# v beside a block of ones in one product with phi(k), and n of chunks 4 to 7 turned by VectorE and DRAM instead of TensorE

## Chip, cores and metric

The kernel runs on one core of a Trainium2 chip. The metric is the device time of one execution in microseconds (us), as the median of the timed executions; smaller is better.

## The reference

One block of a transformer, in float32, for S = 2048 rows, D = 512 columns, H = 32 heads of 16 and a hidden width F = 1376. `mod` holds six vectors made from a small input `c`.

```python
h = layernorm(x) * (1 + ca) + sa
q, k, v = split(h @ wqkv)                       # 32 heads of 16
phi(t) = concat(softmax(t @ w_phi), softmax(-t @ w_phi))      # 32 features a head
kv = phi(k)^T v ;  z = sum over the rows of phi(k)            # a head: 32 x 16, and 32
o = (phi(q) kv) / (phi(q) . z + 1e-6)
x = x + ga * (o @ wo)
h = layernorm(x) * (1 + cb) + sb
n = layernorm(h)
x1 = h + shifted(gelu(n @ w1)) @ w2             # column quarters shifted by +1, -1, +2, -2 rows
x = x + gb * (x1 + gelu(layernorm(x1) @ w3) @ w4)
```

## The kernel before

The 2048 rows are 16 tiles of 128 rows, in 8 chunks of two tiles. Large products are made of three float32r matmuls each (high times high, high times low, low times high), so each operand is split into a high and a low part by `hi_lo` (an ACT or VectorE copy and a subtraction).

**Stage 1, the loop over chunks of lines 802 to 826.** For each chunk `h_chunk` makes h turned (feature by row) with TensorE transposes, `k_feat`, `v_feat` and `q_feat` make a tile's phi(k), v and phi(q) (phi(q) goes to DRAM), and `kv_add` (line 783) adds phi(k)^T v of a tile into the PSUM tile `kva`. There, an item is 32 columns of v (two heads) against 64 columns of phi(k) (their features): 16 items a tile, on the four 32-column strips of the array, each in float32 and so two matmul instructions. Half of each product belongs to two different heads and is masked away later with `block` (line 840). The sum z is made apart: line 790 adds phi(k) of the tiles 0 to 14 into `za` on VectorE or GpSimd, and lines 844 to 847 sum `za` and phi(k) of tile 15 over the partitions by two sets of matmuls with ones; `zbc` holds z on all partitions. `kvb` (lines 833 to 840) is kv turned by matmuls with the identity.

**Stage 2, `phase_a` for each chunk** (line 909) and `mix` (line 1009). `q_phi` loads phi(q), multiplies by `zbc` (tiles `ez`), sums, divides and turns it by VectorE (`pT`). The products `num` (phi(q) kv, 64 x 32 strips of the array), `o` (with wo), two layernorms (tiles `h`, `n`), then n is turned by `to_T` (line 861: four 128x128 TensorE transposes a tile into PSUM `pt`, and `hi_lo` from there into `nT`), then `g` (with w1, gelu) and in `mix` the product `x` with w2. Beside it `split_w3` prepares combinations of w3 and stores them to DRAM.

**Stage 3, `block`**: the last MLP by a Strassen-like scheme: products `u` (with w3, PSUM `pa`) and `b` (with w4, PSUM `ac`). Its operand is turned in another way, by `normed` (line 1118): VectorE turns 32x32 blocks (`turn`), `store_rows` writes the two tiles to DRAM, and `load_turned` fetches them back with the blocks in place, in four DMAs. For that, the ACT pass that normalises writes its columns in a permuted order (`mixed`).

**What sets the order.** Every operation gets a number as the Python code creates it. `ORDER` (line 40) lists these numbers: it is the order in which operations are emitted, and so the order of each engine's own queue (a letter behind a number picks the engine where there is a choice). `SLOT` gives each tile its buffer. The costs that stand beside the operations in the code have no effect when the kernel runs; only these two tables have. The SP queue issues nearly all DMAs, in the same order. So an instruction that waits holds up everything that stands behind it on its engine.

On TensorE, with a name for each operation by its step and tile (k, v, q, kv of tiles 0 to 15; num and g of chunks 0 to 7, o, n and x by tile; z, kvb, w2: small products on strips of the array), the order before has the strip products in these runs: w2; kv0 to kv3; kv4 to kv6; kv7; kv8 to kv11; both z and kv12 to kv14; kv15; kvb; num0; num1 in two runs; num2 to num7 in one run each. From z to num0 it reads: z z kv12 kv13 kv14 q8 v15 q9 kv15 q12 kvb q10 num0.

Of the kernel before, what the change touches and what calls it, by code (L numbers as in the profile page):

```python
# [11 lines left out]
OP = mybir.AluOpType  # L12
# [3 lines left out]
P = 128  # L16
NK = D // P
HG = 64 // DH
# [16 lines left out]
        "s4": ("mod2", "ke", "qe", "e", "ez", "pT", "gf", "gg", "bH", "bL", "wr", "za", "tw"),  # L35
        "s2": ("raw", "rk", "ws", "tr", "cu", "mod", "acc", "bd", "xl", "xn", "h", "n", "xb", "xc", "gb", "vv", "kvs", "qt", "yt", "sg", "gl", "uu", "nb"),
# [128 lines left out]
)  # L165
SLOT = {
    "pp": "510234426360573046405216574732325716511600313075732270653365216523706542035040435752736700267672"
          "4243153510404460571",
    "bd": "46",
    "w": "134625cd387165ad28cb09",  # L170
    "rk": "73958dgc",
# [1216 lines left out]
```

## Time and profile before

| | us |
|---|---|
| median of 3 timed executions | 554.73 |
| lowest, highest | 554.42, 555.75 |
| profiled execution, first to last instruction (span) | 552.9 |
| median less span: what lies around the first and last instruction | 1.8 |
| TensorE (PE) busy in the span | 544.9 |
| VectorE (DVE) | 488.6 |
| ScalarE (ACT) | 351.7 |
| GpSimd (POOL) | 344.5 |

The profile gives no time of its own for the profiled execution beside its span; the three timed executions stand for it. In the profile, a line such as `L471` is the line of the kernel; `mms` at 471 emits nearly all matmuls, so groups are told apart by their tiles (`kva<-ke,vv` is the sum of phi(k)^T v, `pt<-const,n` the transposes of n). The span falls into three parts: 0 to about 160 us is stage 1, 160 to about 345 us stage 2 with the first products of stage 3 mixed in, and the rest stage 3.

### The profile page before, as it was taken

Reading aid. Unit: us, or ns where it says so; the run is one execution under the profiler, and the core shown is the slowest. Engines: PE = TensorE matmul, PEld = TensorE weight load, DVE = VectorE, ACT = ScalarE, POOL = GpSimd, SP = SyncE. Lnnn points to the kernel's source line nnn. Section 1 sums busy time; section 2 is a strip of 40 time slices with the busy share of each in tenths; the row PEclk is TensorE's granted clock in tenths of the full one; section 3 lists DMA queues with packets and bytes.
Section 4 is the critical chain, followed back from the end, with each engine's and each line's share of the span. In section 5 each row is a group of like instructions: output and inputs, shape, how many; then the busy total and the mean of one; then the engine's idle time right before and its main releaser. Section 6 shows DMA issues by size and latency. Waiting matters only on the chain.

```text
span 552.9 us, 12370 instructions
## 1 busy us (share of the span) xinstructions
PE 544.9 (99%) x4498; PEld 488.1 (88%) x4498; DVE 488.6 (88%) x903; ACT 351.7 (64%) x828; POOL 344.5 (62%) x351
## 2 busy tenths in 40 slices
PE   8999999999989999999999999999999999999997
PEld 7888788878767788888889898999999999999996
DVE  3999999899999999999998878987888868896886
ACT  2899898834436788969888877866434543434540
POOL 2499985979599999978886545234150434254442
PEclk9999999999999999999999999999999999999999
DMA  8982544537736766869987878986689673872022
GB/s 323 392 277 89 175 170 137 176 112 248 205 118 226 249 195 206 275 235 319 292 275 270 242 257 301 339 356 231 284 248 347 245 284 97 264 286 80 25 92 95
DMA packets 63749, 124.90 MB, mean 226 GB/s; under 512 B 7140, under 2 KB 26852, under 8 KB 59592
## 3 DMA queue, kind: packets, MB, share of 16 engines
q1 hardware_dynamic: 63400, 124.04, 66.4%
q8 instruction: 35, 0.57, 0.4%
q14 instruction: 26, 0.21, 0.1%
q10 hardware_dynamic: 288, 0.07, 0.1%
HBM read 89.74 MB, written 34.35 MB: 224 GB/s over the span
## 4 chain that ended last, share of the span: by engine, by line
PE 86%; DVE 7%; POOL 3%; DMA 2%; issue 1%; ACT 0%; DVEq 0%; POOLq 0%
PE pp L471 36%; PE pa L471 27%; PE ac L471 20%; PE pt L480 2%; DVE pz L442 2%; DVE q L442 2%; DMA mod<-in_wmod 1%; PE kva L471 1%; POOL qe L420 1%; DVE pT L762 1%; POOL ez L420 1%; POOL e L420 1%; DVE ez L418 1%; DMA const<-in_c 1%; DVE pp L437 0%
## 5 line engine op out<-in xcount | busy, mean ns | idle before, releaser
L471 PE MATMUL pp<-w,hh 128*128 128x512 f32 x576 | 138.8, 397 | 0.0
L471 PEld LDWEIGHTS pp<-w,hh 128*128 128x128 f32 x576 | 106.7, 188 | 26.1 <-issue 1.6
L471 PE MATMUL pa<-bH,wq 128*128 128x256 f32 x840 | 106.7, 281 | 0.0
L471 PE MATMUL ac<-w,gg 128*128 128x256 f32 x840 | 106.6, 281 | 0.0
L471 PEld LDWEIGHTS ac<-w,gg 128*128 128x128 f32 x840 | 103.4, 189 | 1.1
L471 PEld LDWEIGHTS pa<-bH,wq 128*128 128x128 f32 x840 | 103.1, 189 | 0.9
L471 PE MATMUL pp<-w,sh 128*128 128x512 f32 x192 | 49.4, 399 | 0.0
L471 PE MATMUL pa<-nT,w 128*128 128x256 f32 x384 | 48.3, 282 | 0.8 <-DVE nT L418 0.7
L471 PEld LDWEIGHTS pa<-nT,w 128*128 128x128 f32 x384 | 46.8, 188 | 2.5 <-DVE nT L418 1.2
L471 PE MATMUL pp<-w,oT 128*128 128x512 f32 x192 | 47.4, 395 | 0.0
L471 PEld LDWEIGHTS pp<-w,oT 128*128 128x128 f32 x192 | 35.4, 188 | 8.1 <-DVE oT L418 0.7
L401 ACT ACTIVATE gg<-cu 128x256 fp32r<-128x256 f32 (+1 forms) x56 | 19.1, 359 | 35.1 <-PE ac L471 19.7
L471 PEld LDWEIGHTS pp<-w,sh 128*128 128x128 f32 x192 | 34.6, 188 | 7.5 <-issue 0.8
L588 POOL TENSOR_TENSOR rs<-mv,const 128x2 f32<-128x2 f32 x31 | 23.8, 769 | 25.3 <-ACT mv L595 23.7
L401 ACT ACTIVATE cu<-pa 128x512 f32<-128x512 f32 (+1 forms) x42 | 21.5, 519 | 27.6 <-PE pa L471 22.3
L420 POOL TENSOR_TENSOR gg<-cu,gg 128x128 fp32r<-128x128 f32 (+1 forms) x26 | 15.8, 615 | 33.2 <-ACT gg L401 13.9
L420 POOL TENSOR_TENSOR ez<-e,const 128x1024 f32<-128x1024 f32 x12 | 29.2, 2433 | 5.2 <-DMA dram<-qe 5.1
L401 ACT ACTIVATE gg<-sg 128x512 fp32r<-128x512 f32 x38 | 23.1, 624 | 14.0 <-POOL sg L420 6.0
L420 POOL TENSOR_TENSOR e<-e,q 128x1024 f32<-128x1024 f32 x15 | 28.8, 1938 | 0.4 <-DVE q L418 0.2
L418 DVE TENSOR_TENSOR gg<-cu,gg 128x256 fp32r<-128x256 f32 (+1 forms) x54 | 22.1, 416 | 7.6 <-PE ac L471 4.6
L418 DVE TENSOR_TENSOR gg<-sg,gg 128x512 fp32r<-128x512 f32 x36 | 26.0, 722 | 3.0 <-PE ac L471 1.5
L420 POOL TENSOR_TENSOR ke<-ke,k 128x1024 f32<-128x1024 f32 x14 | 27.2, 1952 | 1.2 <-DVE k L445 1.2
(214 smaller groups left out, 1211.5 us busy)
## 6 DMA issues: line engine op xcount, KB each, us to landing
wq<-dram SPq DMA_DIRECT2D x32, 1024.0 KB, 7.8
dram<-ws SPq DMA_DIRECT2D x35, 256.0 KB, 3.1
xl<-in_x SPq DMA_DIRECT2D x32, 256.0 KB, 4.1
dram<-qe SPq DMA_DIRECT2D x16, 512.0 KB, 3.7
e<-dram SPq DMA_DIRECT2D x64, 128.0 KB, 3.2
raw<-in_w SPq DMA_DIRECT2D x18, 256.0 KB, 3.7
mod<-in_wmod SPq DMA_DIRECT2D x16, 256.0 KB, 5.2
dram<-xl SPq DMA_DIRECT2D x16, 256.0 KB, 3.0
```

The source lines that it names most:

```text
L401: nc.scalar.activation(o(), i(), func, **kw)
L418: dve = ("DVE", 71 + 1.04 * o.n + 90 * (isps(a) and isps(b)), lambda: nc.vector.tensor_tensor(o(), a(), b(), op=op))
L420: pool = ("Pool", cost, lambda: nc.gpsimd.tensor_tensor(o(), a(), b(), op=op))
L442: plan.op("DVE", 65 + 1.04 * a.n + 110 * isps(o), lambda: nc.vector.tensor_reduce(o(), a(), axis=AX.X, op=op), [o], [a])
L471: nc.tensor.matmul(o(), a(), b(), start=s, stop=e, **kw)
L480: nc.tensor.transpose(o(), i(), ident())
L588: plan.op("Pool", 540 + 10 * m, lambda: nc.gpsimd.tensor_tensor(r(), v(), mhalf[:, :m](), op=OP.pow), [r], [v, mhalf])
L762: plan.op("DVE", 71 + 1.04 * o.n, lambda: nc.vector.transpose(o(), i()), [o], [i])
```

## The change

**v beside ones.** v lives in one of three buffers `vz` of 32 heads by 32 columns, whose upper 16 columns of each head are set to 1 once by GpSimd; `v_feat` copies v into the lower 16. An item of `kv_add` is now one head: its 32 columns (v and ones) against its 32 features, 32 items a tile on the four strips. Rows 16 to 31 of each head's 32x32 block of `kva` thereby hold z. The 14 additions into `za`, and `za` itself, are gone. `zbc` comes from `kvs`, the copy of the finished `kva`, by 16 items with a 0/1 matrix `pick`, in place of the two sets with ones; `kvb` comes from 8 items, and the mask is applied to a broadcast of its first 16 columns. Where there were 16 buffers for v, `v_feat` of a tile now writes over the buffer of the tile three before it.

**n turned through DRAM.** For the chunks 4 to 7, the ACT pass writes n in the permuted order, and `turned_block` does with n what `normed` did for stage 3: VectorE `turn`, two stores, four loads, into a new tile `zt`. `nT` is split from there instead of from PSUM. 32 of the 64 transposes of n, and 8 PSUM tiles, are gone.

**Order and buffers anew.** `ORDER` and `SLOT` are replaced as a whole. On TensorE the strip products now stand in these runs: w2; kv0; kv1; kv2 and kv3; kv4; kv5 and kv6; kv7 and kv8; kv9 and kv10; kv11 to kv13; kv14, kv15 and z; kvb; num0 to num3 one run each; num4, num5 two runs each; num6; num7 two runs. From z to num0 it reads: z q6 q10 q11 q8 kvb q9 q15 num0. GpSimd's last step for phi(k), the multiplication by the reciprocal sum, stands in the list directly ahead of kv2, kv4 and kv9 with no work for TensorE between. At the start the transposes of the first chunk come ahead of the third and fourth load of `mod`, where one half stood behind the fourth and the other behind a transpose of `mod`. Steps of `split_w3` begin early in stage 1. The cost written beside a matmul on a strip has its floor changed from 56 to 30, without effect when the kernel runs.

```diff
-    kva = T("kva", [P, NG // 2, P // 2])
-    zacc = T("za", [P, 2 * D])
-    first = []
+    kva = T("kva", [P, NG, 2 * DH])
+    plan.at("vz")
+    vz = [T("vz", [P, H, 2 * DH]) for _ in range(BIAS["vz"])]
+    for v in vz:
+        plan.op("Pool", 700, lambda v=v: nc.gpsimd.memset(v[:, :, DH:](), 1.0), [v[:, :, DH:]])
     def kv_add(e, vv, tt_):
         plan.at(f"kv{tt_}")
-        mms([(kva[32 * (g % 4):32 * (g % 4) + 32, g // 4, :], vv[:, 32 * g:32 * (g + 1)], e[:, 64 * g:64 * (g + 1)],
-              tt_ == 0 and g < 4, tt_ == NT - 1 and g > 2 * NG - 5) for g in range(2 * NG)],
-            [kva], [vv, e], skip=True, tiles=4)
-        first.append(e)
-        if tt_ and tt_ not in BIAS["zpe"]:
-            tt(zacc, first[0] if tt_ == 1 else zacc, e, OP.add, "any")
+        items = []
+        for i, a in np.ndindex(NG, 4):
+            h = 16 * (i // 4) + 2 * (4 * (i % 2) + a) + i // 2 % 2
+            items.append((kva[32 * a:32 * (a + 1), i, :], vv[:, h, :], e[:, 2 * DH * h:2 * DH * (h + 1)],
+                          tt_ == 0 and i == 0, tt_ == NT - 1 and i == NG - 1))
+        mms(items, [kva], [vv, e], skip=True, tiles=4)
...
-    mms([(p[64 * (i // 2):64 * (i // 2) + 64, half * (i % 2):half * (i % 2 + 1), :], kvs[:, i, :], ident.re("p (a x) -> p a x", (half, 2 * DH), a=half), True, True)
-         for i in range(half)], [p], [kvs, ident], tiles=2)
+    mms([(p[32 * (i // 2):32 * (i // 2) + 32, 4 * (i % 2):4 * (i % 2) + 4, :], kvs[:, i, :], ident.re("p (a x) -> p a x", (4, 2 * DH), a=4),
+          True, True) for i in range(NG)], [p], [kvs, ident], skip=True, tiles=4)
...
-    parts = [zacc] + [e for t, e in enumerate(first) if t in BIAS["zpe"]]
-    for n, e in enumerate(parts):
-        mms([(p[32 * a:32 * (a + 1)], ones[:, :32], e.re("p (r f a y) -> p r f a y", (2, NG, 2, 2 * DH), r=2, a=2, y=2 * DH)[:, a // 2, :, a % 2], n == 0,
-              n == len(parts) - 1) for a in range(HG)], [p], [ones, e], skip=True, tiles=4)
+    mms([(p[32 * b:32 * (b + 1)].re("p (u a) f -> p u a f", (2, 4, 2 * DH), u=2)[:, :, a, :], pick[:, a, :], kvs[:, 2 * b:2 * b + 2, :], True, True)
+         for a in range(4) for b in range(4)], [p], [pick, kvs], skip=True, tiles=4)
...
+    def turned_block(xs):
+        z, yd = T("zt", [P, CH // 32, NK, 32]), T("dram", [TPC * P, D])
+        for t, x in enumerate(xs):
+            y = T("yt")
+            turn(y, x)
+            store_rows(yd, t, y)
+        load_turned(z, yd)
+        return z
...
             for i, t in enumerate(ts_):
-                act(ns[t], hs[t], scale=r[:, i:i + 1], bias=nmr[:, i:i + 1])
-                sl = slice(t * P, (t + 1) * P)
-                to_T(ns[t], nT[:, 0, :, sl], nT[:, 1, :, sl])
+                if c not in BIAS["nturn"]:
+                    act(ns[t], hs[t], scale=r[:, i:i + 1], bias=nmr[:, i:i + 1])
+                    sl = slice(t * P, (t + 1) * P)
+                    to_T(ns[t], nT[:, 0, :, sl], nT[:, 1, :, sl])
+                    continue
+                act(*mixing(ns[t], hs[t]), scale=r[:, i:i + 1], bias=nmr[:, i:i + 1], alts=("DVE",))
+        if c in BIAS["nturn"]:
+            z = turned_block(ns)
+            zp = z.perm("p a k j -> p k a j", (1, 0, 2))
+            for j in range(2):
+                ks = slice(2 * j, 2 * j + 2)
+                hi, lo = (nT[:, i, ks, :].re("p k (a j) -> p k a j", (2, CH // 32, 32), j=32) for i in range(2))
+                hi_lo(hi, lo, zp[:, ks], lo_eng="either")
```

More of the change, by code (lines that the diff above doesn't have):

```diff
@@ new lines @@
+    "xn": "200b19hcab3k6263",
+    "mod": "0ea58dgi94hlka0ib1",
+    "mod2": "0123",
+    "kva": "0",
+    "vz": "381",
+    "hh": "487487de",
+    "pt": "126534152332132374573543",
+    "raw": "b67bg2d1aichdcl9463h94e3kjek",
+    "k1": "0044322032214153",
+    "ke": "5029675064907640",
+    "k2": "1042434324123520",
+    "qe": "7469560119615037",
+    "q1": "2000400051320334",
+    "qt": "a42784d07e4g",
+    "acc": "d162k",
+    "kvs": "g",
+    "pz": "0",
+    "q2": "01200023",
+    "e": "5279860289382068",
@@ new lines @@
+    "ez": "0303338367779393",
+    "q3": "3300002222330000",
+    "q5": "35423333",
+    "pT": "1557381068933276",
+    "oT": "87d11444",
+    "nT": "0de77ee0",
+    "n": "4gac9a49818kk5f5",
+    "h": "87d06bf2d31ab82c",
+    "gf": "70779559",
+    "sh": "501e1379",
+    "pa": "464747424205037245173231047014523646712756343651442037660205",
+    "wr": "24645",
+    "ws": "748b4e4f8hb0j35ab48egi7141a560iafc2",
+    "zt": "7775",
+    "yt": "1e785fhhakifigh4a11f28fe",
+    "gb": "l",
+    "tw": "13741",
@@ new lines @@
+    "bL": "26030597",
+    "nb": "8a1ifid7d79dfkk6",
+    "bH": "89840482924568142417091818628684",
+    "tr": "5ig1fc1h4jk4bi83",
+    "wq": "5705e5ea7b5a7bcba5ba75c7ba5bac5bc7a5",
+    "cu": "i60574abk2dj03ig827fcbea6j9d4117205fa894",
+    "gl": "e1hk2h17",
+    "ac": "62535123354017207651157320417356",
+    "gg": "39765216478519407260923746819347693250691847230456453214092376513427059634817620",
+    "sg": "h1hgch2ceca5e4c4fd0h883fcgf4eiikj6dh3ki6",
+    "xb": "89k961705kbcg93a",
+    "xc": "gdbeabdia3kekdjh",
@@ L226 @@
+    "uu": "319gie11",
 }
@@ L229 @@
 BIAS = {"start": 1, "late": 2, "ln_act": [1, 2, 3, 4, 5, 6, 7], "pair": [0, 1, 2, 3, 4, 5, 6, 7], "qpool": [0, 2, 4,
-        6, 8, 9, 10, 11, 12, 13, 14, 15], "tw": "any", "zpe": [15]}
+        6, 8, 9, 10, 11, 12, 13, 14, 15], "tw": "any", "vz": 3, "nturn": [4, 5, 6, 7]}
 class Tl:
@@ L464, in mms @@
             else:
-                cost, rec, duty = cost + 2 * max(56 if tiles > 1 else 110, 4 + 0.8333 * b.n) / tiles, rec + 2, min(0.5, 0.004 * b.n)
+                cost, rec, duty = cost + 2 * max(30 if tiles > 1 else 110, 4 + 0.8333 * b.n) / tiles, rec + 2, min(0.5, 0.004 * b.n)
         def fn():
@@ L749, in v_feat @@
         plan.at(f"v{tt_}")
-        vv = T("vv")
-        p = proj(rows(hh, t), w, vv, parts=parts)
+        vv = vz[tt_ % len(vz)]
+        p = proj(rows(hh, t), w, parts=parts)
         marks["v"] = marks["proj"]
-        act(vv, p, alts=("DVE",))
+        act(vv[:, :, :DH], heads(p), alts=("DVE",))
         return vv
@@ L907, in q_phi, with store_rows, load_turned, fn @@
         return turned
+    def store_rows(dst, t, i):
+        plan.op("SP", 475, lambda: nc.sync.dma_start(dst()[t * P:(t + 1) * P, :], i()), [dst[:, t * P:(t + 1) * P]], [i],
+                lat=P * D * 4 / 380., land=1500 + P * D * 4 / 300.)
+    def load_turned(o, src):
+        def fn():
+            for b in range(NK):
+                nc.sync.dma_start(o()[32 * b:32 * (b + 1)].rearrange("p a k j -> p a (k j)"),
+                                  src().rearrange("(a i) (b f) -> b i a f", i=32, b=NK)[b])
+        plan.op("SP", 4 * 475, fn, [o], [src], lat=QB * D * 4 / 380., land=4500)
+    def mixing(o, i):
+        return (o.re("p (b k j) -> p k b j", (NK, NK, 32), k=NK, j=32), i.re("p (k b j) -> p k b j", (NK, NK, 32), k=NK, j=32))
+    def turned_block(xs):
[6 more added lines that the diff above has]
+        return z
     def phase_a(c):
```

98 lines of the change are left out of this document (22 added, 76 removed), and 244 rows, old and new, of the table ORDER.

## The prediction

> **What bounds the kernel now.** I read the head of the page first: the span and each engine's busy time.
>
> ```profile
> span 552.9 us, 12370 instructions
> ...
> PE 544.9 (99%) x4498; PEld 488.1 (88%) x4498; DVE 488.6 (88%) x903; ACT 351.7 (64%) x828; POOL 344.5 (62%) x351
> ```
>
> TensorE is busy in 544.9 of 552.9 us. An edit can then bring something in two ways only: less work for TensorE, or fewer of the few gaps. Since matmuls overlap, busy time can hide gaps, so I next split the span by stage (columns: stretch, its length, then busy us and instructions of each engine, granted clock, DMA share, GB/s).
>
> ```profile
> 13.80:27.60 13.80, 13.80 (x90) 12.26 (x89) 13.41 (x23) 11.82 (x35) 6.09 (x8) 1.00 1.04 392
> 27.60:142.60 115.00, 115.00 (x884) 92.66 (x882) 110.48 (x153) 86.48 (x193) 97.78 (x70) 1.00 0.53 173
> 142.60:209.80 67.20, 64.68 (x645) 51.95 (x652) 66.02 (x102) 42.05 (x93) 61.51 (x39) 1.00 0.64 200
> 210.00:340.00 130.00, 130.00 (x1079) 114.40 (x1059) 119.16 (x211) 107.51 (x269) 96.29 (x106) 1.00 0.83 271
> 340.00:520.00 180.00, 180.00 (x1481) 178.00 (x1481) 148.85 (x335) 92.42 (x217) 66.60 (x104) 1.00 0.69 242
> ```
>
> From 13.8 us on, TensorE has a gap in one stage alone: 142.6 to 209.8 us, where phi(q) is divided and the first chunks of stage 2 run. There VectorE is busy 66.02 of 67.20 us, so it is as full as TensorE. Who holds TensorE up is in the groups of its instructions (busy us, mean ns of one, idle before and what ended it):
>
> ```profile
> L471 PE MATMUL pa<-nT,w 128*128 128x256 f32 x384 | 48.3, 282 | 0.8 <-DVE nT L418 0.7
> ...
> L471 PE MATMUL pp<-pT,const 64*32 64x128 f32 x512 | 9.4, 274 | 1.7 <-DVE pT L762 1.7
> ```
>
> The first `num` waits 1.7 us for VectorE's turned phi(q), and a `g` waits 0.7 us for `nT`. With 67.20 less 64.68, the gaps of the stage are 2.5 us.
>
> **The change part by part: TensorE's own work.** The chain of waits runs along TensorE nearly throughout, so its pieces (start, us, what) are prices of TensorE work.
>
> ```profile
> 10.82 0.64 PE pp L471 x8
> 11.46 0.58 PE pt L480 x4
> 12.04 0.36 PE pp L480 x2
> 12.40 0.44 PE pt L480 x4
> ...
> 89.38 2.79 PE pp L471 x12
> ...
> 315.92 0.87 PE pt L480 x8
> ...
> 352.93 0.71 PE ac L471 x6
> ```
>
> Twelve 512-column matmuls take 2.79 us (0.2325 each), six 256-column ones 0.71 (0.118 each), and a transpose 0.87 / 8 = 0.109. The chunks 4 to 7 lose 4 x 2 x 4 = 32 transposes: **-3.5 us**.
>
> The products on strips are dearer to enter than to run. TensorE's timeline around z (start, us from first start to last end, what):
>
> ```profile
> 142.68 0.64 PE L471 MATMUL pp<-za,const 128*32 128x256 f32 x8
> 143.13 0.61 PE L471 MATMUL pp<-ke,const 128*32 128x256 f32 x8
> 143.56 1.52 PE L471 MATMUL kva<-ke,vv 128*32 128x64 f32 x96
> 145.02 8.61 PE L471 MATMUL pp<-w,hh 128*128 128x512 f32 x36
> 153.56 0.65 PE L471 MATMUL kva<-ke,vv 128*32 128x64 f32 x32
> 154.14 3.05 PE L471 MATMUL pp<-w,hh 128*128 128x512 f32 x12
> ```
>
> From start to start, three `kv` take 145.02 - 143.56 = 1.46 us and one takes 154.14 - 153.56 = 0.58, so one more `kv` in a run costs (1.46 - 0.58) / 2 = 0.44, and a run has 0.14 fixed. The 36 matmuls behind it take 153.56 - 145.02 = 8.54 where 36 x 0.2325 is 8.37: another 0.17. A run of strip products thus costs 0.31 us beside its work. The order before has 17 runs and the new one 22: **+1.5 us**.
>
> The two z sets take 143.56 - 142.68 = 0.88. The new set has 32 instructions of 64 columns, as many as one `kv` before, 0.44: **-0.4 us**. `kvb` has twice the items on twice the strips, no change.
>
> Now `kv` itself. Before, 32 instructions of 64 columns on four strips, eight rounds of four: 0.44 / 8 = 0.055 us a round. After, 64 instructions of 32 columns, sixteen rounds. A round of 256 columns took (143.13 - 142.68) / 2 = 0.225, four times that of 64 columns, so down to 64 columns the price is proportional to the columns, and 32 give 0.028. From below the issue bounds it; the windows of the instructions on `kva` show the first four matmuls and loads of a run issued within 0.025 us:
>
> ```profile
> 72.80:72.83 0.03, 0.02 (x4) 0.02 (x4) 0.00 (x0) 1.00 0.00 0
> ```
>
> Both say 0.028 to 0.03 a round, so 0.45 to 0.48 a tile where it was 0.44: **+0.4 us** over 16 tiles. The upper end is a price by instruction, 0.055 a round: 16 x 0.44 = +7.0. I take the lower end because the row of 256 columns leaves no fixed part. The Trainium skill speaks against it: its page TensorEngine Tiling (Array Packing), section Performance Considerations, says that each matmul has about 60 cycles of overhead, that one of a single column takes as long as one of 60, and not to tile a dimension that is already small. By that page the upper end holds; no row here has fewer than 64 columns on a strip.
>
> Sum of TensorE's work: -3.5 + 1.5 - 0.4 + 0.4 = **-2.0 us**.
>
> **The start.** Before, TensorE waits for the fourth `mod` load until 10.82, and then come 0.58 + 0.44 us of transposes of the first chunk. The new order puts them ahead of the third and fourth load, into that wait: -1.0 at best, 0 if the folding of weights behind them then waits for its loads instead (the DMA runs at 392 GB/s from 13.8 to 27.6, share 1.04, so it is full). I take **-0.5**.
>
> **The other engines in stage 1.** The additions into `za` and the last step of phi(k):
>
> ```profile
> L420 POOL TENSOR_TENSOR ke<-ke,k x14: 1933/1942/1999, 43.5 to 135.9; 128x1024 f32<-128x1024 f32 x14
> L420 POOL TENSOR_TENSOR za<-za,ke x8: 2388/2400/2463, 70.1 to 137.9; 128x1024 f32<-128x1024 f32 x8
> ```
>
> Eight of the 14 additions take 8 x 2.40 = 19 us of GpSimd, and six more stand on both engines. TensorE never waits in 27.6 to 142.6, so they are worth nothing there; the new order spends the room on `split_w3`. What is new is a wait: ACT's copy of v waits for the `kv` of three tiles earlier, and behind it in ACT's queue stand the exponentials and the copies of h, for which TensorE's next products wait. The PSUM bank of that v is held meanwhile. And `kv` now has little room behind GpSimd's multiplication of 1.94 us: three of them (kv2, kv4, kv9) follow it in the list with no TensorE work between. Nothing in the trace shows such a wait. Its bounds are 0, if GpSimd runs ahead, and 3 x 1.94 = 5.8; I take **+0.4**, nearer to 0, because GpSimd has 17 us free in that stage. The three fills of `vz` fall into the start, where GpSimd is free for 7.7 of 13.8 us, and cost nothing. ACT's copy of v has as many elements as before; that they land in strides is taken at nothing, since ACT is free for 28 us of the stage.
>
> **From z to the first chunks.** z now needs the last `kv`, and so all of k and v. In return, six projections and `kvb` stand between z and the first `num`: 6 x 2.79 = 16.7 us of cover and a little for `kvb`. Before, VectorE was busy throughout between the two (busy us in the order PE, PEld, DVE, ACT, POOL):
>
> ```profile
> 142.70:162.50 19.80, 18.08 (x217) 13.85 (x217) 19.40 (x24) 6.85 (x13) 14.53 (x8) 1.00 0.52 157
> ```
>
> Its new list in between is about those 19.4 us, less a subtraction, a split and one `ez` that go elsewhere, plus four sums and a second chunk's division: by estimate 17 to 19 us. So the wait of 1.7 ends between 0 and 1.8. The wait for `nT` should go: where `g` followed the transposes of n directly, half an `o` or a whole `g` half (2.8 us) stands between now. Of 2.5 us I take **-1.5**; the ends are -2.5 and +1.
>
> **n turned through DRAM.** The same route exists in stage 3 (VectorE's turn and the landings of its two stores; then, by the tile that they load, the four loads, the split into high and low part, and their landings):
>
> ```profile
> L762 DVE STREAM_TRANSPOSE yt<-nb x16: 668/704/712, 261.3 to 377.5; 128x512 f32<-128x512 f32 x16
> ...
> DMA to landing us min/median/max: 2.0/2.9/6.4
> ```
> ```profile
> L1111 SPq DMA_DIRECT2D bL<-dram x32: 302/447/1357, 267.1 to 470.6; - x32
> L401 ACT ACTIVATE bH<-bL x15: 614/622/634, 281.3 to 508.2; 128x512 fp32r<-128x512 f32 x15
> L418 DVE TENSOR_TENSOR bH<-bL,bH x13: 677/685/1052, 283.0 to 509.3; 128x512 fp32r<-128x512 f32 x13
> ...
> DMA to landing us min/median/max: 2.4/3.2/6.2
> ```
>
> From the second turn to a complete `nT`: 0.70 + 2.9 + three more issues of 0.447 + 3.2 + 0.62 + two subtractions of 0.685 = 10.1 us. By the new order TensorE has in that time, for chunk 4, eight quarters of `x` (24 x 0.2325), two halves of `o` (12 x 0.2325) and the `num` of a chunk (9.4 / 8): 5.6 + 2.8 + 1.2 = 9.6 us; for chunk 6, two halves of `g` and three `u` (48 and 36 x 0.118): 9.9 us. Chunks 5 and 7 have some more. The turn may come early or late against that list, so the cover is just enough at median landings; at the slowest ones (6.4 and 6.2) up to 6.5 us a chunk would stand open. The two stores and four loads a chunk sit in SP's queue, and while a load waits for its stores, everything behind it waits: loads of later x rows, the ring of w3, stores of w3 parts. These have long leads. In all 4 MB (half written, half read) are added to 271 GB/s over 130 us, or 35 MB: share 0.83 goes to about 0.93, still below the full 1.04, but landings get longer. VectorE gains 8 x 0.70 = 5.6 us of work where it has 10.8 us free. I take **+0.4**, ends 0 and +10.
>
> **Sum.** -2.0 - 0.5 + 0.4 - 1.5 + 0.4 = -3.2 us. The profiled span would be 549.7; the median stands 1.8 above the span, and goes from 554.73 to **551.5**. Stage 3 from 340 us on has no gap and keeps its work.
>
> **The rivals.** (1) A strip product of 32 columns costs as much as one of 64. For: the trace has none shorter, and weights must be reloaded twice as often. Against: the proportion from 256 to 64, and eight instructions issued in 0.025 us. It adds 7.0 - 0.4 = 6.6: **558.1**, slower. It decides from the point where a round costs 0.028 + 3.2 / 256 = 0.041 us. This is the result that the page's rule would give. (2) The new couplings take the gain: `kv` behind GpSimd, `g` of chunks 4 and 6 behind DRAM. For: covers of 9.6 and 9.9 us against 10.1. Against: GpSimd's free time, and the row of 210 to 340, where the same route already runs without a gap. Two `g` that open by 1 us and two `kv` by 0.8 take about 3: **554.7**, no change. Should the landings go toward their slowest under the added traffic, it is 3 to 6 us more, and slower. (3) All gaps close, the start gives its 1.0 and nothing new opens: -2.0 - 1.0 - 2.5 = -5.5, **549.2**. (4) The change doesn't do what it says: extra runs cost more than 0.31 because they now stand alone, which eats the -2.0; it ends as (2) does.
>
> **How the numbers follow.** A measurement of this kernel can tell about 0.3% from no change, 1.7 us: faster is below 553.1, slower above 556.4. The forecast has 0.45 and (3) 0.14, both faster: 0.59. (2) with (4) has 0.23 for no change and 0.06 for its slower end; (1) has 0.12: slower 0.18. The range leaves out (1) at its full price and the best of (3): 548.8 to 557.0. The likeliest sign's own range is 548.8 to 553.
>
> **What would show it.** Right: 32 transposes of n; 1024 matmuls `kva<-ke,vz` at some 0.46 us a tile within a run; no wait of the first `num` over 1 us; no `za`. Wrong: `kv` near 0.9 us a tile (rival 1); TensorE waiting in stage 1 for GpSimd's `ke`, or for `nT` between 210 and 345 us (rival 2); a first `num` that waits longer than 1.7 us, which would make the order around z worse and not better.

## The result, and the profile after

| | before | after |
|---|---|---|
| median, us | 554.81 | 595.14 |
| lowest to highest, us (4 runs each) | 554.42 to 555.75 | 594.55 to 599.98 |
| span of the profiled execution, us | 552.9 | 593.8 |

The ratio is 1.0739 (95% interval 1.0698 to 1.078): **40.3 us slower**, where 3.2 us faster was forecast. The profiled execution of after took 595.62 us itself, so 1.8 us lie around its span as before. Here and below, a run more than 1.5% above the fastest of its kernel is left out: one of spread_psum (599.34 us) and one of before_new_order (690.55 us). Lines of after are lower by four: `mms` is L467, where it was L471.

The head of the page of after:

```profile
span 593.8 us, 13462 instructions
...
PE 560.6 (94%) x5002; PEld 490.3 (83%) x5002; DVE 510.5 (86%) x904; ACT 340.2 (57%) x788; POOL 363.0 (61%) x387
```

TensorE's busy time grew by 15.7 us (544.9 before) and its idle time from 8.0 to 33.2. Busy time is no measure of its work here, since overlapping matmuls hide short gaps and a lower clock stretches them. What shows the change of nature is the chain of waits. Its shares in before:

```profile
PE 86%; DVE 7%; POOL 3%; DMA 2%; issue 1%; ACT 0%; DVEq 0%; POOLq 0%
```

and in after:

```profile
PE 21%; DVE 14%; DMA 13%; ACT 7%; issue 5%; POOL 4%; SPq 3%; DVEq 0%; POOLq 0%; ACTq 0%
```

The chain that ends last ran along TensorE for 86% of its span; now it changes engine all the time, and 13% of the span are spent in transfers. By stage (columns: stretch, its length, busy us of PE, PEld, DVE, ACT, POOL, granted clock, DMA share, GB/s), after:

```profile
13.80:27.60 13.80, 13.80 (x100) 12.36 (x93) 11.63 (x22) 11.34 (x30) 3.61 (x5) 1.00 1.01 356
27.60:142.60 115.00, 110.06 (x1165) 87.38 (x1164) 107.95 (x146) 80.14 (x179) 87.38 (x85) 0.99 0.54 174
142.60:209.80 67.20, 63.77 (x791) 49.51 (x790) 60.84 (x94) 32.48 (x72) 58.94 (x36) 0.97 0.45 143
210.00:340.00 130.00, 121.38 (x1007) 101.52 (x1006) 111.70 (x185) 103.31 (x245) 101.06 (x103) 1.00 0.83 268
340.00:520.00 180.00, 172.99 (x1341) 165.47 (x1339) 151.83 (x312) 86.49 (x204) 76.74 (x109) 1.00 0.78 264
520.00:593.80 73.80, 65.95 (x525) 63.84 (x525) 63.10 (x135) 22.79 (x56) 30.40 (x39) 1.00 0.31 108
```

Before, 142.6 to 209.8 us was the only stage after the start with a gap up to 520 us. Now every stage from 27.6 us on has gaps: 4.9, 3.4, 8.6, 7.0 and 7.9 us. Of the 7.9, 3.8 lie behind the last matmul, as in before. The last two stages lie, but for the 17 us until the last `g`, where the change leaves the computation as it was. No other engine is the bound: VectorE is busy for 86% of the span. The waits of TensorE in after (released tile, by what; sum us, count, largest):

```profile
PE pa L467 <- DVE xb L414: 4.0, 4, 1.9
PE kva L467 <- DVE vz L406: 3.5, 1, 3.5
PE pp L467 <- DVE oT L414: 3.5, 3, 2.1
PE pp L467 <- DVE h L433: 2.0, 4, 0.8
PE pa L467 <- DVE nT L414: 1.9, 2, 1.2
```

There is no large one. The two that were feared are nearly absent: `nT` has 1.9 us, and the first `num` no wait at all (in the timeline, a wait would stand in brackets behind the row; two later `num` wait 1.4 us together):

```profile
179.65 1.16 PE L467 MATMUL pp<-pT,const 64*32 64x128 f32 x64
```

What leads the list is one late copy of v and, in stage 3, the x rows `xb`, followed back in the chain of after (start, us, what):

```profile
397.58 7.62 DMA xb<-dram
...
405.94 1.00 DVE xb L414
406.97 1.51 DVE xb L414 x3
408.47 0.04 issue
408.52 8.79 PE pa L467 x72
```

A load of 7.62 us, then VectorE's split, then at once the 72 matmuls that need it. Landings of these loads from 400 to 560 us, before:

```profile
xb<-dram SPq DMA_DIRECT2D x12, 256.0 KB, 3.1
...
wq<-dram SPq DMA_DIRECT2D x14, 1024.0 KB, 6.1
```

and after:

```profile
xb<-dram SPq DMA_DIRECT2D x11, 256.0 KB, 7.2
...
wq<-dram SPq DMA_DIRECT2D x18, 1024.0 KB, 7.0
```

The last figure is the median landing where the trace resolves it. In after, 11 of the 16 loads of `xb` are issued within 5 us behind a 1 MB load of weights (`wq`) on SP's queue; in before, 5 of 16. That the place behind `wq` goes with the long landing shows best within one trace, that of before_new_tail (an experiment below): six `xb` loads behind `wq` landed in 5.4 to 7.5 us, four others in 2.6 to 3.8.

**Where the 40 us lie.** For every matmul I took the distance of its start from the one before, less the median distance of its kind in the profile of before; the sums of these excesses are lost time (idle, or at a lower clock), and the rest is work. Split at TensorE's own milestones, in us, good to about 2 us a row:

| lost until | first kv | first num | last g | last b | sum | work |
|---|---|---|---|---|---|---|
| before | 6.2 | 8.6 | 9.2 | 0.5 | 24.5 | 524.3 |
| after | 13.5 | 11.6 | 22.6 | 17.1 | 64.8 | 525.0 |

The work is the same within that. All of the loss is time in which TensorE stands or runs slowly: 7.3, 3.0, 13.4 and 16.6 us more. The largest part is in the last stretch, whose computation the change leaves as it was.

### The profile page after: what moved, and what is told of

Same layout as the page of the kernel before. It is cut to its first block, busy times and chain, and to the rows that moved or that the text cites. A ratio compares the mean times of both kernels' runs of the same rounds, so it can differ in the third digit from the quotient of the medians.

```text
span 593.8 us, 13462 instructions
## 1 busy us (share of the span) xinstructions
PE 560.6 (94%) x5002; PEld 490.3 (83%) x5002; DVE 510.5 (86%) x904; ACT 340.2 (57%) x788; POOL 363.0 (61%) x387
## 4 chain that ended last, share of the span: by engine, by line
PE 21%; DVE 14%; DMA 13%; ACT 7%; issue 5%; POOL 4%; SPq 3%; DVEq 0%; POOLq 0%; ACTq 0%
PE pa L467 10%; PE ac L467 8%; DVE xb L414 3%; ACT nb L397 3%; PE pp L467 3%; DMA xb<-dram 2%; DVE gg L414 2%; DMA e<-dram 2%; DMA dram<-h 2%; DMA bL<-dram 2%; DVE sg L414 2%; DMA xl<-dram 1%; ACT n L397 1%; DVE yt L758 1%; POOL ez L416 1%
## 5 line engine op out<-in xcount | busy, mean ns | idle before, releaser
L467 PE MATMUL pp<-w,hh 128*128 128x512 f32 x576 | 142.3, 403 | 2.7 <-issue 1.5
L467 PEld LDWEIGHTS pp<-w,hh 128*128 128x128 f32 x576 | 108.2, 191 | 30.3 <-issue 3.9
L467 PE MATMUL pa<-bH,wq 128*128 128x256 f32 x840 | 108.3, 283 | 7.3 <-DVE xb L414 4.0
L467 PEld LDWEIGHTS pa<-bH,wq 128*128 128x128 f32 x840 | 102.7, 188 | 11.5 <-DVE xb L414 4.9
L467 PE MATMUL ac<-w,gg 128*128 128x256 f32 x840 | 107.7, 282 | 2.4 <-DVE gg L414 1.8
L467 PEld LDWEIGHTS ac<-w,gg 128*128 128x128 f32 x840 | 103.8, 188 | 4.8 <-DVE gg L414 2.7
L467 PE MATMUL pp<-w,oT 128*128 128x512 f32 x192 | 48.2, 400 | 5.1 <-DVE oT L414 3.2
L467 PE MATMUL pa<-nT,w 128*128 128x256 f32 x384 | 48.7, 283 | 1.9 <-DVE nT L414 1.9
L467 PE MATMUL pp<-w,sh 128*128 128x512 f32 x192 | 49.3, 398 | 1.1 <-DVE sh L414 0.5
L467 PEld LDWEIGHTS pa<-nT,w 128*128 128x128 f32 x384 | 46.6, 188 | 3.5 <-DVE nT L414 2.3
L397 ACT ACTIVATE cu<-pa 128x512 f32<-128x512 f32 (+1 forms) x38 | 19.3, 520 | 51.8 <-PE pa L467 33.4
L467 PEld LDWEIGHTS pp<-w,oT 128*128 128x128 f32 x192 | 35.0, 188 | 15.2 <-DVE oT L414 4.5
L467 PEld LDWEIGHTS pp<-w,sh 128*128 128x128 f32 x192 | 34.8, 188 | 9.9 <-issue 1.4
L416 POOL TENSOR_TENSOR ez<-e,const 128x1024 f32<-128x1024 f32 x14 | 34.5, 2476 | 5.0 <-issue 2.8
L416 POOL TENSOR_TENSOR ke<-ke,k 128x1024 f32<-128x1024 f32 x16 | 31.2, 1963 | 5.0 <-DVE k L441 4.1
L397 ACT ACTIVATE gg<-cu 128x256 fp32r<-128x256 f32 (+1 forms) x51 | 17.3, 359 | 17.8 <-PE ac L467 10.1
L416 POOL TENSOR_TENSOR e<-e,q 128x1024 f32<-128x1024 f32 x13 | 26.1, 2020 | 1.1 <-DVE q L414 1.0
L414 DVE TENSOR_TENSOR gg<-cu,gg 128x256 fp32r<-128x256 f32 (+1 forms) x58 | 24.3, 432 | 1.7 <-ACT cu L397 0.8
L397 ACT ACTIVATE cu<-cu 128x512 f32<-128x512 f32 (+1 forms) x36 | 19.7, 550 | 9.9 <-DVE cu L414 8.3
```

Source lines behind the costliest of these rows:

```text
L397: nc.scalar.activation(o(), i(), func, **kw)
L414: dve = ("DVE", 71 + 1.04 * o.n + 90 * (isps(a) and isps(b)), lambda: nc.vector.tensor_tensor(o(), a(), b(), op=op))
L416: pool = ("Pool", cost, lambda: nc.gpsimd.tensor_tensor(o(), a(), b(), op=op))
L467: nc.tensor.matmul(o(), a(), b(), start=s, stop=e, **kw)
```

## The experiments

Each has the kernel before on the same chip beside it (555.01, 555.21, 554.94, 555.00, 554.62 and 555.34 us in the six sets). "Lost" and "work" are sums as in the table above.

### Each half of the change alone, in the old order

**v beside ones alone (v_old_order).** All edits around `vz`, `kva`, z and `kvb`, except that v has 16 tiles here, each filled with ones by GpSimd (16 fills of 0.53 us), and not three buffers filled once; the list of before, with z behind kv15 and some v and kv steps moved. The `kv` stand in eight runs here, in six in before.

```diff
-    "vv": "3246ekjhkfh0170l",
+    "vz": "9472278304072738",
...
-    zacc = T("za", [P, 2 * D])
...
+        vv = T("vz", [P, H, 2 * DH])
+        plan.op("Pool", 700, lambda: nc.gpsimd.memset(vv[:, :, DH:](), 1.0), [vv[:, :, DH:]])
```

> Only the v part of the change (16 tiles of v with ones in buffers shared with other tiles, product with phi gives the sum, no sums on VectorE), in the order of before; n is turned by TensorE as before. Theory O: 550 to 560 (within 1 percent of before). Theory C with the v part as the costly one: 570 or more. If this is at 555 and the kernel with the whole change in the old order is far above, the way through DRAM is what costs.

576.05 us, ratio 1.0371 (1.0314 to 1.0429); the profiled execution took 571.30. Its work is 528.4, 4.1 more than before (good to about 2), so this half makes TensorE's work larger, not smaller. Lost: 37.0, with 16.8 (8.6 before) until the first `num`. The delay against before is 16.7 us at the first `nT` and stays so to the end.

**n through DRAM alone (t_old_order).** `turned_block` and the list of before, the turns put where the transposes stood. `SLOT` differs only by the places of the new tiles `zt` and `yt`; the eight changed buffers that the expectation speaks of are not in it.

```diff
-        6, 8, 9, 10, 11, 12, 13, 14, 15], "tw": "any", "zpe": [15]}
+        6, 8, 9, 10, 11, 12, 13, 14, 15], "tw": "any", "nturn": [4, 5, 6, 7], "zpe": [15]}
```

> Only the second part of the change, in the order and on the engines of before: n of the last four chunks goes through VectorE and DRAM, v and the sums are as before. The first use of chunks 4, 6 and 7 stands 4, 3 and 3 us later; 8 old tiles change buffers. The kernel with both parts in this order lost some 40 us between 250 and 385 us, with TensorE waiting for nT. Theory L (each turn, store and load takes some 7 us longer than the four transposes, and TensorE has little else to do there): 580 to 597. Rival (what was lost there came of the 171 tiles whose buffers had changed): 555 to 570.

595.82 us, ratio 1.0735 (1.0714 to 1.0755). The work is 520.8: 3.5 less, as the 32 transposes were priced (good to about 2). But 69.2 us are lost, 53.8 of them between first `num` and last `g`. TensorE's waits, and its timeline at the two largest (start, us, what, and the wait ahead of it):

```profile
PE pa L471 <- ACT nT L401: 24.3, 2, 15.3
PE pa L471 <- DVE bH L410: 6.7, 1, 6.7
```

```profile
266.84 0.58 PE L471 MATMUL pa<-nT,w 128*128 128x256 f32 x1 [8.95 <-ACT nT L401]
...
324.38 5.78 PE L471 MATMUL pa<-nT,w 128*128 128x256 f32 x24 [15.34 <-ACT nT L401]
```

From the end of VectorE's second turn to the start of the split stand 6.4 and 6.9 us for chunks 4 and 5 in this trace (7.0 and 7.5 to the second half's split), although the loads themselves land in 2.3 to 3.2. The list of before left the transposes right ahead of `g`, and this latency now lies on TensorE's path. But for chunk 6, which has the largest wait, it is 13.3 us, and the excess isn't DRAM's: the four loads were issued by 314.4 us, and ScalarE, which is to split what they bring, stood first for a load of x rows:

```profile
320.78 0.63 ACT L401 ACTIVATE nb<-xl 128x512 f32<-128x512 f32 x1 [5.97 <-DMA xl<-dram]
...
323.72 0.61 ACT L401 ACTIVATE nT<-zt 128x512 fp32r<-128x512 f32 x1
```

So the 24.3 us are not all latency of the turn; part is an engine that waits, in its own order, for something else.

**One chunk through DRAM (turn_one).** Chunk 5 only, where the old list leaves some 9 us between n and its use.

```diff
-        6, 8, 9, 10, 11, 12, 13, 14, 15], "tw": "any", "zpe": [15]}
+        6, 8, 9, 10, 11, 12, 13, 14, 15], "tw": "any", "nturn": [5], "zpe": [15]}
```

> The kernel before with the second part of the change for chunk 5 alone, nothing moved later: its 8 transposes on TensorE go (0.9 us), its n goes through VectorE and DRAM. The order leaves 9.0 us of TensorE work between the second turn and the first use of nT in this chunk, and 5 to 6 us in chunks 4, 6 and 7. In t_old_order a hi part starts 7.0 to 7.5 us after the end of the turn of chunks 4 and 5, and hi and lo of both halves take 2.5 to 3.5 us more. Theory L (the way through DRAM costs what its latency exceeds the work that stands in between): 554 to 558. Rival (the store and the loads disturb SP's queue wherever they stand): 562 or more.

560.15 us, ratio 1.0072 (1.0047 to 1.0096): 4.8 us slower. The latency is mostly covered here, and 0.9 us of transposes (a quarter of 3.5) are gone, yet it doesn't pay. The lost time rises by 6.6, all of it between the first `num` and the last `g`. TensorE's largest new wait there isn't for the turned chunk, but for an n of a chunk that TensorE still turns, which is late on GpSimd:

```profile
PE pt L480 <- POOL n L410: 2.3, 1, 2.3
```

So a chunk whose own latency is covered seems to push others back on the engines that it shares with them. Not all of the 6.6 us belongs to it: 1.7 stand behind the 1.72 us wait of the first `num`, which before has too, and come of a granted clock of 0.50 from 164.0 to 167.4 us, where before's trace has 1.00. At like clock the run is 3.4 to 4.1 us slower (558.34 against 554.95 us at mean clocks of 0.999 and 1.000; 560.26 against 556.13 at 0.997 and 0.996). The time ended 2 us above the range expected from latency alone.

**Both halves in the old order (all_old_order; all_old_wide).** The second delays the first use of the turned n by up to 8 us of TensorE's work in the list, against the latency (chunks 4 to 7: by 4, 0, 3, 3 us in the first; 8, 2, 8, 7 in the second).

```diff
-ORDER, SLOT of after
+ORDER, SLOT of before, with the changed steps put in their place
```

> The whole change (v tiles with ones, no sums on VectorE, n of the last four chunks through DRAM), but every operation that both kernels have stands in the order, on the engine and as far as possible in the buffer of the kernel before; the new operations stand where the old ones stood, the k-v products somewhat earlier, and the first use of the turned n of chunks 4, 6 and 7 some 3 to 4 us later so that its loads have time. Theory O (the new order with its engines and buffers costs the 40 us, not the work that is changed): 550 to 563. Theory C (the changed work itself costs them, by the v tiles or by the way through DRAM): 585 to 600. In between (565 to 585): both.

> As the whole change in the old order (612), with the first use of the turned n of chunks 4, 6 and 7 some 8, 8 and 7 us later than in the kernel before instead of 4, 3 and 3 (that of chunk 5 2 us later), which is the 7 us that the trace of that kernel shows from the end of a turn to the first use of what was loaded. Theory L (the way through DRAM costs by its latency where TensorE has nothing else to do): 580 to 595. Rival (the transfers themselves, or the order's fit, cost): 605 to 620.

612.44 (ratio 1.1040; 1.1021 to 1.1058) and 625.30 (1.1266; 1.1235 to 1.1298). Two theories fell here. That the changed work would be fast if only the old order were kept: it is slower than after, by 17 us. And that more distance heals it: in the second the wait for `nT` is small, and others lead:

```profile
PE pp L469 <- DVE pT L760: 13.2, 2, 11.9
PE pp L469 <- POOL sh L1041: 12.0, 2, 9.5
PE pp L469 <- DVE h L416: 6.8, 1, 6.8
PE pa L469 <- ACT nT L399: 4.3, 2, 3.6
```

What is put off in the list puts off what stands behind it. The halves add up nearly: 20.8 + 41.2 = 62.0 where both cost 57.2 (with three `vz` buffers in place of 16 tiles).

### The old work with one piece of the new list

**z behind the last kv (before_late_z).** The change needs this order: z comes from the finished `kva`. Here it is made in the kernel before; with z move the steps that need it, and seven tiles take other buffers for it.

```diff
-657 295 683 584 1481 381 684 797 603 685
+657 295 584 1481 381 797 603
...
-798 654 466 587
+798 654 683 684 685 708 706 799G 709 707 710 711 712 713 714 717G 466 587
```

> The kernel before with all its work; only the two products that make the sum z over phi of k, and its copy, stand behind the last k-v product instead of some 11 us ahead of it, and what needs z follows it in the order; seven tiles change buffers for that. Theory Z (what costs in the v part is that z comes with the last k-v product, so that the chain z, phi of q, first numerator starts later than TensorE can bridge): the first numerator 11 to 15 us later, total 565 to 572. Rival V (it is the 16 tiles with ones and the wider products): 554 to 558.

565.50 us, ratio 1.0188 (1.0171 to 1.0205): 10.6 us slower with the same work. The timeline of TensorE in this run:

```profile
153.91 0.61 PE L470 MATMUL pp<-za,const 128*32 128x256 f32 x8
...
170.27 1.96 PE L470 MATMUL pp<-pT,const 64*32 64x128 f32 x64 [8.78 <-DVE pT L761]
```

z starts 11.2 us later than in before (142.68), and the first `num` waits 8.78 us for the phi(q) that is divided by it. In all_old_order the same wait for `pT` is 11.9 us. In v_old_order, where more projections stand ahead of it, the first `num` waits 1.6 us, so how much of its 20.8 this dependency is was not separated.

**The new tail (before_new_tail), the old tail (after_old_tail).** Up to about the start of stage 3 one list, from there the other's order, engines and buffers; the computation behind the cut is the same in both.

```diff
 ORDER[:1788] of before
-ORDER[1788:] of before
+the same steps in the order of after
```

```diff
 ORDER[:1668] of after
-ORDER[1668:] of after
+the same steps in the order of before
```

> The kernel before as it is up to its 1788th operation, and behind it, for the same work, the order, the engines and the preferred buffers of the changed kernel; no work is changed at all. Theory O: 565 to 573, since the last 200 us take the 14 us that the changed kernel lost there. Theory C: 553 to 558.

> The changed kernel as it is up to its 1668th operation (all of k, v, q, the sums and all n), and behind it the order, the engines and the preferred buffers of before; the work behind this point (u, a, the products with w3 and w4) is the same in both kernels. Theory O: the last stage gives its share back, 575 to 584. Theory C: what is lost in the last stage is carried over from the changed work ahead of it, so 590 to 600.

583.16 us (ratio 1.0506; 1.0479 to 1.0533) and 604.26 (1.0886; 1.0832 to 1.0939). The old work with the new tail lost 28 us in the tail alone. So the new list costs in a stage whose work is the same. But the old tail behind the new front doesn't heal it: it is 9 us slower than after. A tail seems to fit only the front that it was made with. (182 and 227 tiles had to take other buffers, which is a cost of its own, below.) The waits of the first:

```profile
PE pa L470 <- DVE xb L417: 9.4, 3, 5.4
```

The same x rows as in after lead. Around the largest of its gaps:

```profile
496.00:501.90 5.90, 5.72 (x46) 5.32 (x45) 5.28 (x10) 2.25 (x5) 1.91 (x3) 1.00 0.94 332
501.90:507.40 5.50, 0.33 (x3) 0.12 (x2) 5.46 (x9) 1.18 (x3) 5.34 (x7) 0.86 0.17 69
507.40:511.00 3.60, 3.39 (x16) 3.42 (x17) 0.99 (x3) 0.00 (x0) 1.10 (x2) 0.50 0.19 73
511.00:516.00 5.00, 5.00 (x38) 5.00 (x38) 1.23 (x3) 0.13 (x1) 0.00 (x0) 0.83 0.89 291
```

A gap can have a second price: behind this one the granted clock is 0.50, and the 23 matmuls from 507.61 to 512.65 us stand 0.213 us apart in place of 0.119, another 2.2 us on a gap of 5.4. In after, the single late copy of v does the same: the wait of 3.5 us for `vz`, then the stretch behind it at half clock:

```profile
75.60:77.60 2.00, 1.99 (x69) 1.94 (x70) 1.94 (x3) 0.00 (x0) 0.00 (x0) 0.50 0.36 134
```

The length of the gap alone doesn't decide it. In after, the clock is 0.50 from 160.7 to 164.1 us behind a gap of only 1.50 us:

```profile
160.66 12.71 PE L467 MATMUL pp<-w,hh 128*128 128x512 f32 x47 [1.50 <-issue]
162.40:164.10 1.70, 1.70 (x5) 1.34 (x4) 0.64 (x1) 0.00 (x0) 1.70 (x2) 0.50 0.59 204
```

The 1.72 us wait of the first `num` has 0.50 behind it in turn_one and 1.00 in before, and in after_early_loads a gap of 3.51 us (up to 51.86 us) has 1.00 behind it. The Trainium skill's page TensorE: Matmul & The Clock Gate, section HAM oscillation — how this bites in real kernels, gives the rule that idle gaps must stay below about 3.4 us. The gaps of 3.5 us in after and of 5.4 agree with it; those of 1.50, 1.72 and 3.51 us do not.

**Engines alone (before_tail_engines, after_old_engines).** Letters of the list only: 190 in the tail of before set as in after, and all 384 that differ in after set back.

```diff
-1727 1729G 1717 1751G
+1727G 1729 1717V 1751
```

```diff
-49 41 48 58V 2753G
+49V 41V 48G 58 2753
```

> The kernel before, order and buffers untouched; from its 1788th operation on the 190 operations that the changed kernel gives to another engine are given to that one. With order, buffers and engines of the changed kernel this stage took 28 us more. Theory E (the engines: 38 operations from ScalarE to VectorE against 21 back): 570 to 585. Rival B (order and buffers): 554 to 562.

> The changed kernel, order and buffers untouched; all 384 operations that it gives to another engine than the kernel before does are given back. Theory E: 575 to 585. Rival B: 590 to 600 (or more, since engines and order no longer fit).

559.95 us (ratio 1.0086; 1.0069 to 1.0103) and 671.45 (1.2086; 1.2058 to 1.2114). The new engines in the old tail cost 5 us; the old engines in the new order cost 76 more than it does. The engines seem to fit the order that they came with.

**The whole new order with the old work (before_new_order).** The list of after with the old steps put in for the changed ones; 288 tiles take other buffers.

```diff
-ORDER, SLOT of before
+ORDER, SLOT of after, with the old steps put in their place
```

> The work of the kernel before, all of it (v without ones, sums on VectorE, n turned by TensorE), in the order and on the engines of the changed kernel throughout, with its buffers preferred; 64 of 203 loads stand under 1 us ahead of their first use, as in the changed kernel. It is the fourth corner beside old work in old order (555), new work in old order (612) and new work in new order (595). Theory O (the new order costs by itself, whatever work it holds): 585 to 615. Theory W (the new order is as good as the old one, and only the changed work needs the time): 555 to 570.

681.5 us (679.75 and 683.18); ratio 1.2278 (1.2227 to 1.2328). 153 us are lost, in every stage (24.5 in before). With all_old_order this makes a square: old work and old order 555, new work and new order 595, the two mixed pairs 612 and 681. Work and order belong together, and no statement "the order costs so much" can be made apart from the work.

### Loads and buffers

**Loads late (before_late_loads).** In after, 66 of 207 loads stand less than 1 us of TensorE's work ahead of their first user in the list, and none of 203 in before. Here 64 loads of before are moved back to so short a lead.

```diff
 ORDER, position of a load's word (`xb`, `xc`, `wq`):
-1761: 1677
-1762: 1803
-1843: 1944
+1761: 1736
+1762: 1888
+1843: 2014
```

> The kernel before with its buffers, its engines and its order on the other engines; only the 64 loads that stand under 1 us ahead of their first use in the changed kernel are put right ahead of their first use here too. Theory P: 575 to 600, most of what the changed kernel lost, without any changed work. Rival B: 554 to 560, since SP still issues a load as soon as its buffer is free and nothing ahead of it in the queue waits.

654.23 us, ratio 1.1795 (1.1766 to 1.1824): 99 us slower, by nothing but the place of 64 loads. Its largest wait:

```profile
PE pa L470 <- DMA wq<-dram: 13.0, 2, 7.6
```

**Loads early (after_early_loads).** In after, 101 loads moved forward, until one is left under 1 us; two tiles change buffers.

```diff
 ORDER, position of a load's word (`xb`, `wq`, `wq`):
-1765: 1852
-1840: 1863
-1839: 1874
+1765: 1838
+1840: 1844
+1839: 1848
```

> The changed kernel with the same work, engines and order on TensorE, VectorE, ScalarE and GpSimd; only loads are moved forward in the order of the DMA queue. In the kernel before, each of 203 loads into a tile stands at least 1.8 us of TensorE work ahead of its first use (201 of them 3 us or more); in the changed kernel 66 of 207 stand under 1 us ahead of it. Here 101 loads are put forward until they stand about 6 us ahead, as far as their buffer allows (1 is left under 1 us); two tiles change buffers. Theory P (the new order places loads too late in SP's queue, behind stores that wait for their data): 570 to 582. Rival B (what costs is when buffers come free and the order on the other engines): 590 to 600.

629.08 us, ratio 1.1346 (1.1315 to 1.1377), 34 us slower than after. The theory that late loads are what ails after failed in this form. TensorE's waits:

```profile
PE pp L470 <- DVE oT L417: 10.4, 3, 6.0
...
PE pa L470 <- DVE xb L417: 3.8, 3, 1.9
```

The waits for `xb` are what they were (4.0 in after), so the place of the word in the list is not what makes them late; those for `oT` rose from 3.5 to 10.4. That loads listed earlier wait in SP's queue for their buffers, and hold up what stands behind them, is a likely cause but is not shown: the queue waits for VectorE's `gg` 31.0 us in ten times here, and 27.9 in seven times in after.

**Buffers dealt anew.** Only `SLOT` is changed. before_tight gives each tile the lowest free buffer, before_lru the one longest free; spread_all, spread_psum and spread_sbuf deal the tiles of after to the buffer longest free, in all memories, in PSUM only (206 tiles) and in SBUF only (834). The first twelve places of `pp` in before_tight, then in spread_all and spread_psum:

```diff
-510234426360
+000000405300
```

```diff
-000000440300
+534021364562
```

and of `h` in before_lru, then in spread_sbuf:

```diff
-7519l62c7i1l
+ihbe8gd7ji18
```

```diff
-87d06bf2d31a
+g5kbij96hc58
```

> The kernel before with its order kept word for word and SLOT dealt out tightly: each tile gets the lowest free buffer of its class. Nothing else changes, no part of the change is in it. Theory B: 575 to 600 us, as slow as the changed kernel. Theory O: 554 to 560 us.

> The kernel before with its order and engines, every tile dealt anew to the buffer of its class that has been free the longest; that is the control for the kernels in which buffers were dealt anew. Theory P: 554 to 562 (dealing as such costs little as long as buffers have been free for long). Rival B: 580 or more.

> The changed kernel with its order kept word for word and only the buffer table SLOT dealt out anew: each tile gets the buffer of its class that has been free longest, in PSUM and in SBUF. Theory B (the new SLOT hands a buffer on right behind its last reader, and these new waits cost the time): back to 552 to 565 us. Theory O (the new order itself, with kv tied to three v buffers and n through DRAM, costs it): 585 us or more, as the changed kernel's 595.

> The same, with only the eight PSUM banks dealt out anew and SBUF as in the change. Theory B: a good part of the loss comes back, 565 to 580 us, since 85 of 225 PSUM handovers lie within 1 us of TensorE work in the changed kernel against 16 of 233 before. Theory O: 588 us or more.

> The same, with only the SBUF buffers dealt out anew and PSUM as in the change. Theory B: what the PSUM part leaves, 570 to 585 us. Theory O: 588 us or more.

| | us | ratio (95%) |
|---|---|---|
| before_tight | 669.80 | 1.2069 (1.2012 to 1.2127) |
| before_lru | 569.30 | 1.0257 (1.0207 to 1.0307) |
| spread_all | 609.89 | 1.0990 (1.0958 to 1.1022) |
| spread_psum | 589.28 | one run, no interval |
| spread_sbuf | 607.50 | 1.0947 (1.0885 to 1.1009) |

My first theory was that after loses because its buffers are dealt tightly. Tight buffers do cost, 115 us in the old order; but spreading them in after made it 12 to 15 us slower, save in PSUM, where the one run is 6 us faster; that shows little, since the runs of after itself spread from 594.55 to 599.98. Even the rule that sounds safest, the buffer longest free, costs the old order 14 us.

## Why the prediction was wrong, point by point

**The step that failed** is the assumption under the whole sum, put most plainly as "Stage 3 from 340 us on has no gap and keeps its work" (and for stage 1 as "TensorE never waits in 27.6 to 142.6"). I priced the changed instructions and the couplings named in the diff, and took the replaced `ORDER` and `SLOT` as neutral wherever the work stayed. The trace of before could not show that: it shows that the old list has no gap. Stage 3 did keep its work and lost 16.6 us more; before_new_tail shows that the new tail costs there even with the old work in front (28 us, with 182 tiles in buffers of neither list). In after, some 24 of the 40 us lie where the sum had put nothing or a gain: 2.4 in the first run of matmuls, 3.5 and 1.2 at and behind a late copy of v, 16.6 behind the last `g`. Of the 13.4 between the first `num` and the last `g`, how much is the list and how much the turned n is not separated. Nor is the new list bad by itself: the new work is 17 us slower in the old one.

**TensorE's work**, forecast -2.0, came to +0.7 (good to about 2). By its parts:
- Transposes -3.5: borne out (t_old_order's work is 3.5 less).
- z, the extra runs and `kv`, together +1.5, came to +4.1 in v_old_order. The `kv` term was mis-sized: forecast 0.45 to 0.48 us a tile. TensorE's timeline of after:

```profile
115.53 1.30 PE L467 MATMUL kva<-ke,vz 128*32 128x32 f32 x128
116.81 8.50 PE L467 MATMUL pp<-w,hh 128*128 128x512 f32 x36
...
128.55 1.36 PE L467 MATMUL kva<-ke,vz 128*32 128x32 f32 x128
129.84 8.61 PE L467 MATMUL pp<-w,hh 128*128 128x512 f32 x36
```

Two tiles take 116.81 - 115.53 = 1.28 and 1.29 us; less the fixed 0.14, a tile is 0.57, against 0.44 before. That is 0.125 more a tile and +2.0 over 16, where +0.4 was forecast. A round costs 0.57 / 16 = 0.036 us: dearer than in proportion (0.028), far from 0.055, and below the 0.041 from which rival 1 decides. The rule that the Trainium skill's page TensorEngine Tiling (Array Packing), section Performance Considerations, gives, by which 32 columns would take as long as 60, is half borne out: the price is not in proportion, but at 0.036 it is well below the 0.055 of 64 columns.

**The start**, forecast -0.5, went the other way. TensorE's first run takes, before and then after:

```profile
0.97 7.59 PE L471 MATMUL pp<-const 128*128 128x128 f32 x48 [0.97 <-POOL const L498]
```

```profile
0.97 9.96 PE L467 MATMUL pp<-const 128*128 128x128 f32 x48 [0.97 <-POOL const L494]
```

The same 48 matmuls take 2.4 us longer. In after the first six `pp` tiles all lie in buffer 0, in before in six different ones. The traces of spread_all, which deals after's PSUM anew, and of spread_sbuf, which keeps it, show that this is a cause:

```profile
0.97 7.43 PE L466 MATMUL pp<-const 128*128 128x128 f32 x48 [0.97 <-POOL const L493]
```

```profile
0.97 9.67 PE L466 MATMUL pp<-const 128*128 128x128 f32 x48 [0.97 <-POOL const L493]
```

In all seven traces whose first six `pp` tiles share buffer 0 this run takes 8.9 to 10.1 us, in the thirteen others 7.0 to 8.5. At full clock the matmuls of a tile stand 0.112 us apart in both kernels, but in the shared buffer two steps at each change of tile take 0.33 and 0.21: 0.32 us more. Five changes make 1.6 of the 2.4 us, by estimate. The rest goes with the time from which the trace has the full clock on record, 5.1 us in before and 7.1 in after; it differs between runs of one order too.

**kv behind GpSimd** (+0.4): TensorE's large wait of stage 1 does not lie there, but at the first `kv`, for a copy of v on VectorE: 3.5 us and half clock behind it. TensorE stands from 72.09 us on; ahead of the copy, VectorE's queue holds steps of `split_w3` (`ws`). The new list runs 54 of them before 142.6 us, the old one 36, and the prediction counted the additional ones as free:

```profile
72.36 1.91 DVE L406 TENSOR_SCALAR ws<-ws 128x256 fp32r<-128x256 f32 x1
...
74.79 0.68 DVE L406 TENSOR_SCALAR vz<-pp 128x512 f32<-128x512 f32 x1
```

**Waits from z to the first chunks** (-1.5): right for the first `num`, which waits for nothing in after, and it has the cover that was named (projections): before_late_z shows what the same dependency costs without them, 10.6 us. `nT` still waits 1.9 us.

**n through DRAM** (+0.4, ends 0 and +10): in t_old_order the latency from the end of the second turn to the split is 6.4 and 6.9 us where nothing else intervenes, and the forecast's terms up to there (2.9, three issues of 0.447, 3.2) give 7.4. In after it is 9.1 to 12.2 us, with landings of 2.9 to 6.2, and still the new order covers nearly all of it: `g` waits 1.9 us. Its price shows where it is not covered: 41 us for four chunks, 4.8 for the best-placed one, in each case with what it does to other steps. The end of +10 was taken for the new order, and there the loss between first `num` and last `g` is 13.4; how much of that is the turn was not separated.

**The rivals.** Rival 2, that new couplings take the gain, is the right kind: waits in place of the removed work, in many places. At 554.7, and 3 to 6 us more at its slow end, it was too small by 35 us, because it counted only couplings that the diff names. Rivals 1, 3 and 4 did not happen; 595.14 lies far outside the range.

**What stays open.** Which elements of the new list cost the 16.6 us of the last stretch: `xb` loads that land in 7.2 us behind 1 MB loads and VectorE's split of them lead the waits, and late loads are shown to be dear in the old list, but moving loads forward in the new one cost 34 us, so this is a symptom as much as a cause. The new order with only the transposes of n put back was not tried. No version here is faster than before.

## What to carry to other kernels

A hand-fitted list of order, engines and buffers is a part of the kernel's work: replacing it as a whole costs or gains more than the few microseconds of instructions that a diff counts, so look in it first for loads that stand right ahead of their first user, buffers reused at once, and latencies moved onto a chain. When TensorE is 99% busy, removing 1% of its work pays only if every step that replaces it finds a cover that is already there; a transposition traded for 6 to 12 us of latency, as measured here, wants that much other work between, for each chunk. And a list should be judged by the gaps that its own trace shows, not by those that the old one lacks.

## What the runs showed of the hardware

- After a gap of 3.5 us, and of 5.4, TensorE's granted clock was 0.50, in the second case for 5 us: 2.2 us on top of the gap. It was also 0.50 for 3.4 us after a gap of 1.50 us, and 1.00 after one of 3.51.
- Matmuls of 128x128 in float32 that write one PSUM tile after another stood 0.112 us apart where each tile had its own buffer; where all shared one, two steps at each change of tile took 0.33 and 0.21 us.
- Strip products of 32 columns cost 0.036 us a round of four, those of 64 cost 0.055: these two rows alone would give a fixed part of 0.017 and 0.0006 a column, while 64 and 256 columns (0.225) stand in proportion. The price of one tile rests on the same fixed 0.14 us a run in both kernels.
- In before_new_tail, loads of 256 KB issued within 5 us behind a 1 MB load on the same queue landed in 5.4 to 7.5 us, the others in 2.6 to 3.8.
